# Bucketed attention and a rational feed-forward layer: partial sums merged by an adding transfer, four additions per pair moved to DVE

## The chip, the core and the metric

The kernel runs on one core of a Trainium2 chip. The time is that of the device, in microseconds, from the first to the last work of the core; the median of several runs is compared, and one execution is recorded by the hardware profiler. PE is the engine that multiplies matrices, DVE, ACT and POOL work on tiles of 128 partitions, and SP issues most of the transfers.

## The reference

```python
B, H, S, D = 4, 8, 768, 64
q_bucket = sum((q @ proj > 0) * 2 ** arange(6))        # k_bucket likewise
scores = where(q_bucket == k_bucket, q @ k.T / 8, -1e9)
attn = exp(scores - max(scores))
attn = attn / (sum(attn) + 1e-9)
x = (attn @ v) as (3072 tokens, 512)
h = x @ w_in                                            # 512 -> 2048
P = a0 + a1 h + a2 h^2 + a3 h^3
Q = 1 + |b0| |h| + |b1| h^2
out = (P / (Q + 1e-6)) @ w_out                          # 2048 -> 512
```

Queries see the keys of their own bucket alone. What the change touches is `sum(attn)`: for each query, the sum of the exponentials over all 768 keys, which later divides the values.

## The kernel before

The 32 heads are worked on as 16 pairs (`p`), two heads (`h`) side by side. For a pair the 768 keys are six tiles of 128 (`kt`) and the 768 queries two halves of 384 (`hf`); twelve steps `s` (`hf`, `kt`) make a pair. A step multiplies one tile of keys with one half of the queries, for both heads (`pss`, two products each), ACT takes the exponential into one of seven buffers `E`, and later PE multiplies it with the values (`psv`, twelve products in a row per half). In the same twelve steps PE also makes the twelve products for the maxima of the pair two ahead (`psm`, into two buffers), which DVE reduces one by one (`m`). In every second pair the bucket bits of two coming pairs are made (`psb`, eight products; DVE's comparison `mb`).

The sums over keys have two stages. The six exponentials of a half are added element by element in two parts of three tiles (`PARTS`): `acc = E + E`, then `acc = acc + E`, for each head, so four additions for one part of one half and sixteen for a pair. POOL makes them all, but for nine in the last pairs that DVE makes. A part is one tile `acc` of 128 partitions by two heads by 384, from a pool of five (`ACCS`). Then `sums` lets PE add over the 128 partitions: it multiplies `acc` with a matrix of ones into `psu`, eight products for a pair (two parts, two halves, two heads), the second part added to the first in PSUM. ACT copies the result (`sr`), SP stores it, and after four pairs `recips` reads it back and DVE takes the reciprocals.

Around this the weights of the feed-forward layer are split into two parts (`wr`, `ws`, `wi_hi`, `wi_lo`, on ACT and DVE), and the queries and keys of coming pairs too (`lo` on DVE). The feed-forward layer follows from about 400 us to the end.

Each engine works in the order in which its instructions are written. That order comes from a plan: `at(p, s, f, ...)` puts the call `f` at step 12 p + s, and the calls are made in the order of these numbers. The tables `MID` (pairs in the middle), `FIRST` and `LAST` hold the steps. In `MID`, `sums` stands at 14.65, that is 2.65 steps after the pair's last step, and `sums_store` at 17.37.

Of the kernel before, what the change touches and what calls it, by code (L numbers as in the profile page):

```python
# [7 lines left out]
F32 = mybir.dt.float32  # L8
# [5 lines left out]
ALU = mybir.AluOpType  # L14
# [4 lines left out]
P = 128  # L19
S = 768  # L20
HQ = 384
NT = S // P
# [3 lines left out]
NPAIR = B * NHP  # L26
# [11 lines left out]
PARTS = 2  # L38
ACCS = 5

MID = dict(
    group=6, values=[0.66, 0.05], values_out=3.5, maxima=7.17,
    maxima_steps=[0, 1.15, 1.73, 2.64, 3.32, 5.08, 5.86, 6.98, 8.0, 8.84, 10.26, 11.37], sums=14.65, sums_store=17.37,
    high=[-0.41, 1.19], low=[1.06, 3.35], bits=2.81, penalties=4.05, high_move=1.9, maskrows=5.61, second_low=-2.2,
    second_high=2.69, load_v=10.99, shift_turn=8.61, shift_rows=8.82, load=9.0, recips=[20.0, 22.0, 23.0],
    weights=[[1.44, 4.0, 4.1, 5.09, 5.49, 7.11, 9.5, 9.75, 17.5], [8.05, 10, 10.65, 11.5, 12.38, 14.29, 16.34, 19.32, 21.22]],
    weights_last=[0.5, 0.8, 1.0, 1.2],
)

FIRST = dict(  # L50
    maxima1=4.62, rate1=0.45, maxima2=9.5, rate2=0.82, high=[3.25, 3.53], low=[6.0, 7.3], bits=7.15, penalties=7.25,
    high_move=4.53, maskrows=8.2, second_low=4.25, second_high=4.35, load_v=4.78, group=2,
    values=[2.35, 2.65, 2.32, 2.35, 0.35, 0.61], values_out=3.02, high1=[-0.27, -5.58], low1=[11.24, 4.95],
    high_move1=20.05, load2=21.89, load3=-1.5, penalties1=-6.57, maskrows1=3.69,
    weights=[[-5.7, 6.64, 6.7, 11.42, 12.19, 18.75, 21.75, 38.77, 44.13], [8.03, 9.04, 9.24, 11.12, 14.81, 15.27, 15.99, 17.91, 46.81]],
    warm=6, warms=[3, 3, 3, 1, 1, 1], maxima00=[-4.26, -2.29, -4.17, 1.67, -1.15, 2.77], shift00=[2.15, 4.99],
    shift0=[3.67, 3.44], ahead=3, scores=[[3.68, 3.82, 7.26], [6.03, 8.25, 12.4]], pen01=[4.77, 14.55], comp01=3.35,
    second_high0=[-2.86, 2.12, -3.42, 3.45], load_v0=20.9, bits1=5.23, comp1=[15.82, 11.68],
    maxima0=[3.11, -1.97, -0.5, 2.14, 2.86, 3.25], turn1=[8.46, 13.26], rows1=[9.59, 14.35],
)  # L60

LAST = dict(
    group=6, values=[0.28, 0.44], values_out=1.39, vout14=3.03,
    tokens=[[-7.43, -5.11, -2.83, -1.09], [-0.04, 3.83, 9.38, 9.53]], terms=7.05, ffn=[13.61, 16.09, 16.14],
    sums=16.96, wide=8, share=11, third=0, sums14=14.69, sumst14=22.46,
)
# [99 lines left out]
def attention(ctx, tc, nc, raw, ps_b, tail, tokens, early, operands_to_terms, ffn, load, QF, KF, v, w_in, w_out, wo_d, ident, cst, ones, prj,  # L166
# [9 lines left out]
    sm = ctx.enter_context(tc.tile_pool(name="sm", bufs=1))  # L176
# [169 lines left out]
    def scores(p, s, heads=(0, 1)):  # L346
# [35 lines left out]
    def values_out(p, hf):  # L382
        ps = AV.pop((p, hf))
        col = sm.tile([P, 1], F32, tag="col", name=f"col{p}_{hf}")
        xo = AV[p, hf] = tail.tile([P, HQ], F32, tag="xo", name=f"xo{p}_{hf}", bufs=2)
        nc.scalar.copy(col, ps[:, HQ : HQ + 1])
        nc.scalar.activation(xo, ps[:, 0:HQ], AF.Identity, bias=col)

    def values_store(p, hf):
        nc.sync.dma_start(x_d[p][:, hf * HQ : hf * HQ + HQ], AV.pop((p, hf)))  # L390

    def sums(p):
        ps = ps_b.tile([P, 512], F32, tag="s", bufs=3, name=f"psu{p}")
        for k in range(PARTS):
            for hf in range(2):
                acc = ACC.pop((p, hf, k))
                for h in range(2):
                    o = 64 * h + 32 * hf
                    nc.tensor.matmul(ps[o : o + 32, 0:HQ], ones, acc[:, h, :], start=(k == 0), stop=(k == PARTS - 1))
        ACC[p] = tail.tile([P, HQ], F32, tag="sr", name=f"sr{p}")  # L400
        nc.scalar.copy(ACC[p], ps[:, 0:HQ])
# [69 lines left out]
    def at(p, s, f, *args):  # L471
        plan.setdefault(12 * p + s, []).append((f, args))

    def spread(p, steps, gen):
        for s in steps:
            at(p, s, lambda g: next(g, None), gen)

    for p in range(NPAIR):
        mid = 0 < p < NPAIR - 1
        n = MID["group"] if mid else (FIRST if p == 0 else LAST)["group"]  # L480
        for s in range(12):
            if p > 0 or s >= FIRST["ahead"]:
                at(p, s, scores, p, s)

            if p > 1:
# [8 lines left out]
        if p < NPAIR - 1:  # L494
            at(p, MID["sums"] if p < NPAIR - 2 else LAST["sums14"], sums, p)
            at(p, MID["sums_store"] if p < NPAIR - 2 else LAST["sumst14"], sums_store, p)
        if p > 1:
# [82 lines left out]
    at(0, FIRST["load3"], load, 3)  # L580
    spread(1, (0, 2), coefficients())
    for g in sorted(plan):
# [224 lines left out]
```

## Time and profile before

| | |
|---|---|
| Median of 3 runs | 946.7 us (946.19 to 948.16) |
| Profiled execution | 946.58 us, span 944.8 us |
| PE busy | 935.3 us, 99% |
| DVE busy | 868.6 us, 92% |
| ACT busy | 678.8 us, 72% |
| POOL busy | 442.7 us, 47% |
| Products of the sums (psu) | 256 records of PE, 24.0 us |
| POOL's additions into acc | 247 instructions, 291.1 us |
| DVE's additions into acc | 9 instructions, 10.0 us |
| PE's granted clock | 1.00 in the attention |

An engine's busy time is the time in which at least one of its instructions ran. PE's products overlap, and one product of 32-bit numbers that are not rounded beforehand is two records, so 256 records of psu are 128 products. In the lines of the profile a group reads: line, engine, operation, output and inputs, shape, count, then busy time and mean duration in ns, then the idle time of the engine before it and who ended it. Nearly all instructions carry the line of a helper, so groups are told apart by the names of their tiles. A timeline's row reads: start, duration, engine, instruction, count. A wait's row reads: who waited for whom, total, times, longest.

### The profile page before, as it was taken

The numbers are of one execution on the slowest core, as the hardware profiler recorded it, in microseconds if no ns is written. First come the engines' busy times: TensorE is split into PE (matmuls) and PEld (weight loads), VectorE is DVE, ScalarE is ACT, GpSimd is POOL, SyncE is SP. The second block draws the span as 40 slices with busy tenths as digits, with TensorE's granted clock in tenths as the row PEclk, the third lists the DMA queues.
The fourth block names the chain that finished last, engine by engine and source line by source line (L and its number), as shares of the span: only waits on it lengthen the run. The fifth ranks groups of instructions, "written<-read, shape, count | busy, mean of one in ns | idle before, by whom it ended". The sixth has DMA issues, their size and how long they took to land.

```text
span 944.8 us, 14848 instructions
## 1 busy us (share of the span) xinstructions
PE 935.3 (99%) x5062; PEld 752.0 (80%) x5062; DVE 868.6 (92%) x1217; ACT 678.8 (72%) x1419; POOL 442.7 (47%) x394
## 2 busy tenths in 40 slices
PE   8999999999999999999999999999999999999997
PEld 4666666666667676589989989989899899899996
DVE  6799889888988897899999999999999999999996
ACT  7577767667667676787777787777777777777765
POOL 5587878777778787512222222222222222222222
PEclk9999999999999999999999999999999999999999
DMA  7677878787777767456021021021110110210000
GB/s 212 193 199 207 235 216 239 208 221 221 227 220 225 226 192 215 130 205 252 1 68 34 1 68 34 1 67 34 39 47 17 66 36 1 67 34 1 34 1 34
DMA packets 50032, 111.65 MB, mean 118 GB/s; under 512 B 9154, under 2 KB 22070, under 8 KB 49956
## 3 DMA queue, kind: packets, MB, share of 16 engines
q1 hardware_dynamic: 49524, 110.47, 39.4%
q8 instruction: 40, 0.66, 0.3%
q14 instruction: 36, 0.29, 0.1%
q10 hardware_dynamic: 432, 0.23, 0.1%
HBM read 56.82 MB, written 21.17 MB: 83 GB/s over the span
## 4 chain that ended last, share of the span: by engine, by line
PE 91%; DVE 4%; DMA 2%; ACT 1%; SPq 1%; issue 1%; ACTq 0%; DVEq 0%
PE psh L89 28%; PE pso L89 28%; PE pss L89 12%; PE psv L89 11%; PE psm L89 7%; DVE m L89 2%; PE psu L89 2%; DMA wr<-w_in 2%; PE psb L89 1%; ACT E L89 1%; SPq L89 1%; DVE ws L89 1%; DVE wr L89 0%; DMA kf<-kT 0%; DVE lo L89 0%
## 5 line engine op out<-in xcount | busy, mean ns | idle before, releaser
L89 POOL TENSOR_TENSOR gl<-c,gh 128x384 fp32r<-128x384 f32 x128 | 141.3, 1104 | 395.9 <-ACT gh L89 375.7
L89 ACT ACTIVATE E<-pss 128x384 f32<-128x384 f32 x384 | 167.8, 493 | 108.7 <-PE pss L89 94.6
L89 PE MATMUL pso<-wo,gh 128*128 128x512 f32 x768 | 240.5, 395 | 0.0
L89 DVE TENSOR_REDUCE m<-psm 128x1 f32<-128x768 f32 x192 | 179.5, 948 | 34.3 <-PE psm L89 31.0
L89 POOL TENSOR_TENSOR acc<-E,E 128x384 f32<-128x384 f32 x124 | 154.6, 1267 | 88.6 <-ACT E L89 88.4
L89 PE MATMUL psh<-xl,wi_hi 128*128 128x384 f32 x512 | 172.1, 336 | 0.0
L89 PE MATMUL psh<-xh,wi_hi 128*128 128x384 f32 x512 | 171.7, 335 | 0.0
L89 PE MATMUL pss<-q,k 128*128 128x384 f32 (+2 forms) x768 | 170.9, 346 | 0.7 <-ACT col L89 0.4
L89 PE MATMUL psh<-xh,wi_lo 128*128 128x384 f32 x512 | 171.5, 335 | 0.0
L89 PEld LDWEIGHTS pso<-wo,gh 128*128 128x128 f32 x768 | 142.8, 188 | 23.9
L89 PEld LDWEIGHTS pss<-q,k 128*128 128x128 f32 (+2 forms) x768 | 134.6, 189 | 29.3 <-issue 17.0
L89 ACT ACTIVATE h<-psh 128x384 f32<-128x384 f32 x128 | 63.1, 493 | 126.0 <-PE psh L89 125.9
L89 PE MATMUL pso<-wo,gl 128*128 128x512 f32 x384 | 151.3, 396 | 0.0
L89 DVE SCALAR_TENSOR_TENSOR c<-c,ab,r 128x384 f32<-128x384 f32 x128 | 148.6, 1161 | 0.0
L89 POOL TENSOR_TENSOR acc<-acc,E 128x384 f32<-128x384 f32 x123 | 136.5, 1129 | 7.7 <-ACT E L89 7.5
L89 PE MATMUL psv<-E,v 128*64 128x385 f32 x768 | 133.1, 492 | 0.8 <-ACT E L89 0.7
L89 PEld LDWEIGHTS psv<-E,v 128*64 128x64 f32 x768 | 52.4, 136 | 67.1 <-issue 62.8
L89 PE MATMUL psm<-k,q 76*128 76x384 f32 (+1 forms) x384 | 102.4, 349 | 1.9 <-DVE m L89 1.0
L89 PEld LDWEIGHTS psh<-xh,wi_hi 128*128 128x128 f32 x512 | 96.1, 188 | 6.3 <-issue 1.2
L89 PEld LDWEIGHTS psh<-xl,wi_hi 128*128 128x128 f32 x512 | 96.0, 188 | 5.1
L89 PEld LDWEIGHTS psh<-xh,wi_lo 128*128 128x128 f32 x512 | 96.1, 188 | 0.0
L89 ACT ACTIVATE c<-psh,ab 128x384 f32<-128x384 f32 x128 | 86.5, 676 | 0.4 <-POOL gl L89 0.3
(81 smaller groups left out, 1288.5 us busy)
## 6 DMA issues: line engine op xcount, KB each, us to landing
q<-q SPq DMA_DIRECT2D x45, 192.0 KB
k<-k SPq DMA_DIRECT2D x45, 192.0 KB
wr<-w_in SPq DMA_DIRECT2D x16, 512.0 KB
wr<-w_out SPq DMA_DIRECT2D x16, 512.0 KB
wo_d<-wr SPq DMA_DIRECT2D x16, 512.0 KB
wo<-wo_d SPq DMA_DIRECT2D x16, 512.0 KB
qf<-qT SPq DMA_DIRECT2D x16, 384.0 KB
kf<-kT SPq DMA_DIRECT2D x16, 384.0 KB
```

The source lines that it names most:

```text
L89: return self.tc.keep_in_program_order(issue(*args, **kwargs))
```

## The change

In pairs 2 to 14 (`MERGED`) the two parts of a half are no longer both multiplied with ones. When both are complete, POOL issues a transfer from the second part's tile into the first part's tile that adds (`merge`), two per pair, 128 partitions by 768 numbers each. `sums` then makes four products instead of eight. In the same pairs the last addition of each part for the second head (`kt` 2 and 5, `h` 1) is taken from POOL and made by DVE 1.83 steps after the exponential's step (`add`), four per pair. The first parts have four buffers now and the second parts two, where all shared five; the output tile `xo` of the values has one buffer instead of two.

All tables of the order are rewritten. The sums of a pair stand at 19.5 instead of 14.65 and their store at 23.71 instead of 17.37; pairs 0 and 1 keep the old steps and the eight products, and pair 15 keeps eight products too.

```diff
-ACCS = 5
+ACCS = 4, 2
+MERGED = 2, NPAIR - 1
 MID = dict(
-    ... maxima_steps=[0, 1.15, 1.73, 2.64, 3.32, 5.08, ...], sums=14.65, sums_store=17.37, ... recips=[20.0, 22.0, 23.0],
+    ... maxima_steps=[0.79, 1.23, 1.75, 2.92, 3.18, 5.64, ...], sums=19.5, sums_store=23.71, ... recips=[31.16, 34.8, 44.46],
+    ... merge=[6.88, 7.36], dv=[2, 5], dvlag=1.83,
 ...
-            ACC[p, hf, kt // n] = sm.tile([P, 2, HQ], F32, tag="acc", name=f"acc{p}_{hf}_{kt // n}", bufs=ACCS)
+            ACC[p, hf, kt // n] = sm.tile([P, 2, HQ], F32, tag=f"acc{kt // n}", name=f"acc{p}_{hf}_{kt // n}", bufs=ACCS[kt // n])
 ...
             for h in heads:
-                engine = nc.vector if h and late >= LAST["share"] else nc.gpsimd
-                engine.tensor_tensor(out=acc[:, h, :], in0=x[:, h, 0:HQ], in1=e[:, h, 0:HQ], op=ALU.add)
+                if not (h == 1 and kt in MID["dv"] and MERGED[0] <= p < MERGED[1]):
+                    engine = nc.vector if h and late >= LAST["share"] else nc.gpsimd
+                    engine.tensor_tensor(out=acc[:, h, :], in0=x[:, h, 0:HQ], in1=e[:, h, 0:HQ], op=ALU.add)
+    def add(p, s):
+        hf, kt = divmod(s, NT)
+        acc = ACC[p, hf, kt // (NT // PARTS)]
+        nc.vector.tensor_tensor(out=acc[:, 1, :], in0=acc[:, 1, :], in1=EXP[p, s][:, 1, 0:HQ], op=ALU.add)
 ...
-        xo = AV[p, hf] = tail.tile([P, HQ], F32, tag="xo", name=f"xo{p}_{hf}", bufs=2)
+        xo = AV[p, hf] = tail.tile([P, HQ], F32, tag="xo", name=f"xo{p}_{hf}", bufs=1)
 ...
+    def merge(p, hf):
+        nc.gpsimd.dma_start(ACC[p, hf, 0], ACC.pop((p, hf, 1)), accum_op=ALU.add)
     def sums(p):
-        for k in range(PARTS):
+        n = 1 if MERGED[0] <= p < MERGED[1] else PARTS
+        for k in range(n):
 ...
+            if MERGED[0] <= p < MERGED[1] and s % NT in MID["dv"]:
+                at(p, s + MID["dvlag"], add, p, s)
 ...
+            for hf in range(2 if MERGED[0] <= p else 0):
+                at(p, 6 * hf + MID["merge"][hf], merge, p, hf)
```

On PE, before, in a pair that also makes bits, the four rows of psu (eight products) stand directly ahead of psb:

```order
L89 MATMUL psm_7_1512<-k_5_1225,q_5_1193 128x384 x2
L89 MATMUL psu_1521<-acc_0_0_1216,ones 32x384 x2
L89 MATMUL psu_1521<-acc_1_0_1355,ones 32x384 x2
L89 MATMUL psu_1521<-acc_0_1_1289,ones 32x384 x2
L89 MATMUL psu_1521<-acc_1_1_1427,ones 32x384 x2
L89 MATMUL psb_0_1537<-qf_1134,prj 32x384
```

On PE, now, the sums of a pair:

```order
L92 MATMUL pss_7_1_1340<-q_3_593,k_3_616 128x384
L92 MATMUL pss_7_1_1340<-q_3_891,k_3_892 128x384
L92 MATMUL psm_11_1347<-k_4_897,q_4_875 128x384 x2
L92 MATMUL psu_1355<-acc_0_0_937,ones 32x384 x2
L92 MATMUL psu_1355<-acc_1_0_1084,ones 32x384 x2
L92 MATMUL psm_0_1366<-k_5_1180,q_5_1159 128x384 x2
```

And, further on, the first bits:

```order
L92 MATMUL pss_3_0_1522<-q_4_875,k_4_897 128x384
L92 MATMUL pss_3_0_1522<-q_4_1174,k_4_1175 128x384
L92 MATMUL pss_3_1_1526<-q_4_875,k_4_897 128x384
L92 MATMUL pss_3_1_1526<-q_4_1174,k_4_1175 128x384
L92 MATMUL psb_0_1531<-qf_1091,prj 32x384
```

Four products are left, between two products of maxima, and sums and bits each stand alone.

On POOL, before, one pair's additions (the names are acc with half and part, `x2` is both heads):

```order
L89 TENSOR_TENSOR acc_0_0_934<-E_151,E_152 128x384 x2
L89 TENSOR_TENSOR acc_0_0_934<-acc_0_0_934,E_153 128x384 x2
L89 TENSOR_TENSOR acc_0_1_1018<-E_154,E_148 128x384 x2
L89 TENSOR_TENSOR acc_0_1_1018<-acc_0_1_1018,E_149 128x384 x2
L89 TENSOR_TENSOR acc_1_0_1085<-E_150,E_151 128x384 x2
```

On POOL, now, from the end of one pair into the next:

```order
L92 TENSOR_TENSOR acc_1_1_1148<-E_153,E_154 128x384 x2
L92 TENSOR_TENSOR acc_1_1_1148<-acc_1_1_1148,E_148 128x384
L92 TENSOR_TENSOR acc_0_0_1221<-E_149,E_150 128x384 x2
L92 DMA acc_1_0_1084<-acc_1_1_1148 128x768
L92 TENSOR_TENSOR acc_0_0_1221<-acc_0_0_1221,E_151 128x384
L92 TENSOR_TENSOR acc_0_1_1271<-E_152,E_153 128x384 x2
L92 TENSOR_TENSOR acc_0_1_1271<-acc_0_1_1271,E_154 128x384
L92 DMA acc_0_0_1221<-acc_0_1_1271 128x768
```

Every second row has one addition instead of two, and a transfer stands in POOL's order twice per pair, with the next part's additions behind it.

On DVE, now, from the last maxima of one pair to the first of the next:

```order
L92 TENSOR_REDUCE m_1915<-psm_10_2167 128x1
L92 TENSOR_TENSOR acc_0_1_2108<-acc_0_1_2108,E_148 128x384
L92 TENSOR_REDUCE m_1915<-psm_11_2185 128x1
L92 TENSOR_REDUCE m_2203<-psm_0_2204 128x1
L92 TENSOR_SCALAR mt_None<-pst_None 12x128
L92 TENSOR_REDUCE m_2203<-psm_1_2226 128x1
L92 TENSOR_REDUCE m_2203<-psm_2_2231 128x1
L92 TENSOR_TENSOR acc_1_0_2182<-acc_1_0_2182,E_151 128x384
L92 TENSOR_REDUCE m_2203<-psm_3_2256 128x1
```

Before, no addition stood among these rows; now one stands before the last maximum and one behind the third of the next pair.

More of the change, by code (lines that the diff above doesn't have):

```diff
@@ L38 @@
 PARTS = 2
-ACCS = 5
+ACCS = 4, 2
+MERGED = 2, NPAIR - 1
 MID = dict(
[L42 to L47, printed above, removed]
+    group=6, values=[0.88, 0.46], values_out=3.05, maxima=7.2,
+    maxima_steps=[0.79, 1.23, 1.75, 2.92, 3.18, 5.64, 6.46, 7.46, 9.63, 10.01, 11.6, 12.15], sums=19.5,
+    sums_store=23.71, high=[-1.36, -0.64], low=[2.93, 4.66], bits=3.12, penalties=4.08, high_move=2.8, maskrows=6.75,
+    second_low=-0.71, second_high=6.38, load_v=0.59, shift_turn=8.23, shift_rows=8.41, load=7.35,
+    recips=[31.16, 34.8, 44.46],
+    weights=[[2.04, 4.32, 5.15, 5.84, 6.36, 10.64, 12.29, 15.57, 21.18], [7.54, 10.93, 11.1, 11.86, 12.09, 16.33, 17.02, 18.99, 29.59]],
+    weights_last=[0.5, 0.8, 1.0, 1.2], merge=[6.88, 7.36], dv=[2, 5], dvlag=1.83,
@@ L48 @@
 )
 FIRST = dict(
[L51 to L59, printed above, removed]
+    maxima1=4.33, rate1=0.49, maxima2=9.99, rate2=0.85, high=[2.05, 3.05], low=[4.04, 4.31], bits=5.25, penalties=6.9,
@@ L60 @@
+    shift0=[3.61, 3.85], ahead=3, scores=[[1.64, 4.9, 6.35], [9.05, 9.85, 12.0]], pen01=[6.11, 12.34], comp01=3.58,
+    second_high0=[-0.26, -1.65, -0.72, 7.24], load_v0=21.14, bits1=6.71, comp1=[10.88, 16.35],
+    maxima0=[0.97, -4.4, -0.96, 2.75, 3.35, 3.25], turn1=[7.62, 12.38], rows1=[10.53, 15.94], coef=[-0.5, 20.9],
+    sums=14.65, sums_store=17.37,
 )
@@ L64 @@
     tokens=[[-7.43, -5.11, -2.83, -1.09], [-0.04, 3.83, 9.38, 9.53]], terms=7.05, ffn=[13.61, 16.09, 16.14],
-    sums=16.96, wide=8, share=11, third=0, sums14=14.69, sumst14=22.46,
+    sums=16.96, wide=8, share=11, third=0, sums14=18.5, sumst14=22.46,
 )
@@ L398, in sums @@
                     o = 64 * h + 32 * hf
-                    nc.tensor.matmul(ps[o : o + 32, 0:HQ], ones, acc[:, h, :], start=(k == 0), stop=(k == PARTS - 1))
+                    nc.tensor.matmul(ps[o : o + 32, 0:HQ], ones, acc[:, h, :], start=(k == 0), stop=(k == n - 1))
         ACC[p] = tail.tile([P, HQ], F32, tag="sr", name=f"sr{p}")
```

12 lines of the change are left out of this document (9 added, 3 removed).

## The prediction

> **What bounds the kernel now.** I read the page first (busy shares, slices, chain of waits), then the busy time by stage, then the groups and waits of the stage that the change touches, and last the timeline at the places where the four products of the sums stand.
>
> ```profile
> PE 935.3 (99%) x5062; PEld 752.0 (80%) x5062; DVE 868.6 (92%) x1217; ACT 678.8 (72%) x1419; POOL 442.7 (47%) x394
> DVE  6799889888988897899999999999999999999996
> POOL 5587878777778787512222222222222222222222
> PE 91%; DVE 4%; DMA 2%; ACT 1%; SPq 1%; issue 1%; ACTq 0%; DVEq 0%
> ```
>
> PE is the chain: 91% of it, busy 99% of the span. But DVE stands at eight to nine tenths through the attention (slices 1 to 16) and POOL at seven to eight tenths, so a microsecond taken off PE is worth something only as long as DVE keeps up. The stage with thirteen like pairs shows it. The sums of pair 1 begin at 76.3 us and those of pair 13 at 362.3 us, so this window is twelve pairs (columns: PE, PE's weight loads, DVE, ACT and POOL busy, clock, DMA share, GB/s):
>
> ```profile
> 0.00:52.18 52.18, 49.26 (x258) 29.44 (x259) 37.33 (x54) 32.25 (x57) 30.47 (x37) 1.00 0.70 200
> 76.30:362.30 286.00, 285.70 (x1744) 197.47 (x1743) 254.57 (x298) 199.96 (x450) 226.85 (x193) 1.00 0.76 218
> 362.30:407.90 45.60, 44.18 (x262) 29.67 (x262) 35.20 (x42) 33.41 (x77) 25.99 (x23) 1.00 0.52 160
> ```
>
> 286.00 / 12 = 23.83 us per pair. PE is busy 285.70 of 286.00: it hardly waits. DVE is busy 21.21 us per pair and idle 2.62; POOL is busy 18.90; the DMA engines 0.76 of the time at 218 GB/s. Who waits for whom in that window:
>
> ```profile
> DVE m L89 <- PE psm L89: 22.0, 19, 2.4
> ACT E L89 <- POOL acc L89: 10.7, 4, 3.6
> PEld psm L89 <- DVE m L89: 3.5, 13, 0.5
> ```
>
> DVE waits for PE (22.0 us), and PE's weight loads for DVE only 3.5 us. So PE sets the pace, and DVE follows with little to spare.
>
> **The change, part by part.** *Taken from PE.* A sum of a pair is eight products now (two parts, two halves, two heads), four in the thirteen merged pairs. The timeline of PE shows one beside the bits of a coming pair and one without:
>
> ```profile
> 267.40 1.50 PE L89 MATMUL psu<-acc,ones 128*32 128x384 f32 x16
> 268.72 0.49 PE L89 MATMUL psb<-qf,prj 128*32 128x384 f32 x2
> 291.26 0.51 PE L89 MATMUL psm<-k,q 76*128 76x384 f32 x2
> 291.71 1.50 PE L89 MATMUL psu<-acc,ones 128*32 128x384 f32 x16
> 293.14 0.98 PE L89 MATMUL pss<-q,k 77*128 77x384 f32 x4
> ```
>
> Eight products hold PE for 268.72 - 267.40 = 1.32 us. Half of them go: 0.66 us per pair, 13 x 0.66 = 8.6 us. (Half of the group's busy time would be 0.75; its ends run under the next products, so I take the distance of the starts.) Something comes back: in six places the sums and the bits no longer stand side by side on PE, and each such group alone costs an entry and an exit. Exit: 293.14 - 291.71 = 1.43 instead of 1.32, 0.11 us. Entry: two products of psm take 0.51 us, so the second starts 0.17 after the first, at 291.43, and psu 0.28 later instead of 0.17: 0.11 us. 6 x 0.22 = 1.3 us. PE's own work falls by 7.3 us, 0.56 per pair: PE could run a pair in 23.27 us.
>
> *Added to DVE.* Four additions per pair, 52 in all. DVE makes nine such additions now, in the last pairs, and their groups and three single ones, with the POOL instruction beside the first, read:
>
> ```profile
> L89 DVE TENSOR_TENSOR acc<-acc,E 128x384 f32<-128x384 f32 x5 | 5.6, 1115 | 0.6 <-ACT E L89 0.5
> L89 DVE TENSOR_TENSOR acc<-E,E 128x384 f32<-128x384 f32 x4 | 4.4, 1093 | 1.4 <-ACT E L89 1.4
> 384.58 1.38 DVE L89 TENSOR_TENSOR acc<-E,E 128x384 f32<-128x384 f32 x1
> 384.19 1.35 POOL L89 TENSOR_TENSOR acc<-acc,E 128x384 f32<-128x384 f32 x1
> 386.06 0.56 DVE L89 TENSOR_TENSOR acc<-acc,E 128x384 f32<-128x384 f32 x1
> 388.83 0.55 DVE L89 TENSOR_TENSOR acc<-E,E 128x384 f32<-128x384 f32 x1
> ```
>
> Alone an addition takes 0.55 us (386.06 and 388.83, while POOL stands still); while POOL adds, it waits for POOL to finish and then makes its own (384.58 + 1.38 = 385.96, POOL's ends at 385.54). DVE's instructions overlap by about 0.09 us (176.03 to 176.89 below is 0.86 for 0.95), so the price is 0.46 at least and 1.02 at the mean of the nine. Which, depends on how often POOL is at work. DVE's other work shows what that costs today, in the same window:
>
> ```profile
> L89 DVE SCALAR_TENSOR_TENSOR ws<-ws,wr 128x512 int32<-128x512 int32 x24 | 31.3, 1306 | 0.4
> L89 DVE TENSOR_TENSOR wr<-ws,wr 128x512 fp32r<-128x512 f32 x12 | 17.1, 1425 | 0.0
> L89 DVE TENSOR_TENSOR wi_lo<-ws,wi_hi 128x512 fp32r<-128x512 f32 x12 | 14.0, 1163 | 0.0
> L89 DVE TENSOR_TENSOR lo<-kf,k 128x768 fp32r<-128x768 f32 x12 | 13.6, 1130 | 0.0
> 390.34 0.68 DVE L89 TENSOR_TENSOR wr<-ws,wr 128x512 fp32r<-128x512 f32 x1
> 176.03 0.95 DVE L89 TENSOR_TENSOR lo<-kf,k 128x768 fp32r<-128x768 f32 x1
> 176.89 0.95 DVE L89 TENSOR_REDUCE m<-psm 128x1 f32<-128x768 f32 x1
> ```
>
> With 0.68 as the time alone of the first three and 0.95 of the fourth, DVE stands blocked 24 x 0.63 + 12 x 0.75 + 12 x 0.48 + 12 x 0.18 = 32 us, 2.7 us per pair. POOL's additions read so:
>
> ```profile
> L89 POOL TENSOR_TENSOR acc<-E,E 128x384 f32<-128x384 f32 x97 | 123.4, 1293 | 59.7 <-ACT E L89 59.4
> L89 POOL TENSOR_TENSOR acc<-acc,E 128x384 f32<-128x384 f32 x96 | 107.0, 1135 | 2.0 <-ACT E L89 1.9
> 386.94 1.00 POOL L89 TENSOR_TENSOR acc<-E,E 128x384 f32<-128x384 f32 x1 [1.40 <-ACT E L89]
> ```
>
> Sixteen per pair at 1.00 us alone are 16.0 of 23.8 us, 67%; the change leaves twelve, 12.0 of 23.3, 52%. So a new addition on DVE meets POOL about half the time and then waits half an instruction: 0.46 + 0.52 x 0.5 = 0.72 us, 2.9 per pair; and the old blocked time shrinks with POOL's share, 2.7 x (1 - 52/67) = 0.6. DVE: 21.2 + 2.9 - 0.6 = 23.5 us per pair. The bounds: 21.2 + 4 x 0.46 - 0.6 = 22.4 (every addition alone) and 21.2 + 4 x 1.02 = 25.3 (the mean of the nine, no relief). The middle is already above the 23.27 of PE. The order puts the additions between maxima (behind psm_2, and between psm_10 and psm_11): there PE's next psm needs the maximum behind the addition, two buffers on, so a late DVE is at once a late PE. I take 23.55 us per pair: 0.28 above what PE could do, 13 x 0.28 = 3.6 us given back.
>
> *Taken from POOL, added to it.* Four additions at 1.14 us go, 4.5 us per pair; two issues of a transfer come. No row shows what POOL pays for one. Below, an issue could cost nothing; above, POOL has 23.3 - (18.9 - 4.5) = 8.9 us per pair to give, 4.4 per issue, before it binds. I take it as covered by POOL's idle time. Behind the first transfer of a pair stand the additions of the next half, and the transfer itself waits for DVE's addition; if they are late, the buffers of E are late for ACT. The 10.7 us in four waits of ACT for POOL above cost PE nothing visible (0.30 us idle in the window), so there is cover of that size.
>
> [...]
>
> The slack: the second half's transfer is placed at step 13.36 and the sums at 19.5, a step being 23.8 / 12 = 2.0 us: 12 us. I cost its landing at nothing.
>
> *The transfers' load.* Each carries 128 x 768 x 4 bytes = 393 KB. The engines move 218 / 0.76 = 287 GB/s at full share, so 1.4 us each, 2.7 us per pair; the share rises from 0.76 to (18.1 + 2.7) / 23.3 = 0.89. If an adding transfer moves its bytes twice, 5.5 us: 1.01, no room. No row shows an adding transfer; I take once, and keep twice and more for a rival.
>
> *The rest.* All tables of the order are new, also for pairs 0, 1 and 15, one xo buffer goes, the sums' results come five steps later. PE idles 2.9 us up to 52.18 and 1.4 us from 362.3 to 407.9, so no more than 4.3 us can be won there; as much could be lost. I take nothing. Behind 407.9 the work is untouched.
>
> Sum: -8.6 + 1.3 (entries) + 3.6 (given back by DVE, 13 x (23.55 - 23.27)) = -3.7. The profiled execution took 946.58 us (span 944.8, the rest lies around it), so 942.9; it stands 0.1 under the median of 946.7, so for a median **943.0 us**.
>
> **The rivals.**
>
> 1. *PE keeps all of it* (chance 0.20): DVE's additions fall into its 2.62 us of idle time and POOL's relief pays for their waits (22.4 per pair, under 23.27). For it: DVE waits 22.0 us for PE. Against: those waits stand where the maxima arrive, not where the additions do. 946.6 - 7.3 = 939.3 us.
>
> 2. *No change* (0.18): DVE takes 23.7 to 23.95 per pair, and the gain is eaten. 946 us.
>
> 3. *DVE becomes the bound* (0.25). Place: the maxima that follow an addition. Price: at 1.02 us each, less the 0.6, DVE is 21.2 + 4.1 - 0.6 = 24.7; between that and the 23.83 of today lies 24.3: 13 x 0.5 = +6, 952.6 us (at 24.7: 958). It decides from an addition of 0.8 us on. For it: the mean of all nine rows is 1.1. Against: eight of these stand where POOL adds the other head at the same moment, released by the same ACT.
>
> 4. *The transfers fill the DMA engines* (0.07): at three times their bytes 8.2 us per pair, 26.3 in all, 13 x 2.5 = +32, 979 us at worst; at twice, loads come late by little and the pair stays near 24, 949 us. Against: 0.24 of the time is free today.
>
> **How the numbers follow.** The forecast has 0.30, the largest. About 0.2% (1.9 us) is what can be told from no change. Faster: 0.30 + 0.20 = 0.50; same 0.18; slower 0.25 + 0.07 = 0.32. The likeliest case's own range is 941 to 944.7 (pairs of 23.4 to 23.68 us). For 8 in 10 the range reaches from below rival 1 (938.5) to rival 3 at its middle (952.5), which leaves out half of rival 3 and most of rival 4.
>
> **What would show it.** PE's psu group should fall from 256 to 152 records and by 8 to 10 us busy. DVE's acc group should show 52 more, at 0.55 to 1.4 us, mean near 0.8, and DVE should be busy over 23 us of a pair. The ws and wr groups should come down from 1306 and 1425 ns. POOL's additions should number 16 per pair less four, and ACT's waits for POOL not grow. The DMA share should rise to about 0.89; a rise past 0.95 with waits of ACT or PE for transfers speaks for rival 4. If PE's waits for DVE's maxima stay near 3.5 us, rival 1 is right; if PE's idle or stretched time between psm products passes 0.56 us per pair, rival 3. A POOL row of an issue longer than 4 us, or psu waiting for a transfer, would make the covers wrong that I counted on.

## The result: 36 us slower

The changed kernel takes 983.4 us (median of 4 runs, 981.2 to 990.7) against 947.1 us for the kernel before (946.2 to 948.2). The ratio is 1.040, 95% interval 1.037 to 1.043: slower by 36 us, far outside the range I gave. The profiled execution is one of 981.19 us, with a span of 979.4.

From the page of the changed kernel (engines; slices of DVE, POOL and the granted clock; the chain):

```profile
PE 952.1 (97%) x4958; PEld 755.7 (77%) x4958; DVE 919.4 (94%) x1268; ACT 687.3 (70%) x1419; POOL 386.1 (39%) x369
...
DVE  6889999999999799889999999999999999999997
...
POOL 5676554455565364542222222222222222222222
PEclk9999999999999797999999999999999999999999
...
PE 76%; DVE 12%; issue 5%; DMA 3%; ACT 2%; SPq 1%; POOL 0%; DVEq 0%; ACTq 0%; POOLq 0%
```

PE has 104 records fewer, which are 52 products, as announced, and yet it is busy 17 us longer. The chain of waits shows why to look elsewhere: PE's share fell from 91% to 76%, and DVE's rose from 4% to 12%. In two slices the granted clock stands at 7 tenths, where the windows of before all had 1.00.

Busy time of the eleven pairs from the sums of pair 2 (113.66) to those of pair 13 (406.35), PE, weight loads, DVE, ACT, POOL, clock, DMA share, GB/s:

```profile
113.66:406.35 292.69, 277.68 (x1500) 184.59 (x1500) 275.59 (x316) 189.00 (x410) 157.29 (x154) 0.95 0.83 224
```

Nearly the same stretch of the kernel before, the columns alike:

```profile
100.10:362.30 262.20, 261.90 (x1594) 181.06 (x1592) 234.01 (x275) 183.36 (x413) 208.25 (x177) 1.00 0.77 219
```

292.69 / 11 = 26.6 us per pair, where the eleven pairs took 23.8 each before. DVE is busy 25.05 us of a pair, and PE is idle for 15.0 us of the window, 0.3 before. For whom they wait, in the window of the changed kernel:

```profile
POOL acc L92 <- DVE acc L92: 65.4, 11, 8.1
...
PEld psm L92 <- DVE m L92: 28.3, 37, 2.3
...
PE psm L92 <- DVE m L92: 11.1, 18, 2.0
```

PE's products waited 11.1 us for DVE's maxima, 1.0 us per pair. PE's weight loads waited 28.3 us for them, against 3.5 us in twelve pairs before. The two can't be added: PE as a whole was idle for 15.0. And POOL waits for DVE's addition up to 8.1 us at a time. The groups of DVE's instructions with two inputs in SBUF, POOL's issue of the transfer, and the sums:

```profile
L92 DVE TENSOR_TENSOR acc<-acc,E 128x384 f32<-128x384 f32 x56 | 65.1, 1162 | 1.7 <-POOL acc L92 1.0 <-ACT E L92 0.4
L92 DVE TENSOR_TENSOR lo<-qf,q 128x768 fp32r<-128x768 f32 x13 | 37.1, 2857 | 0.0
...
L92 DVE SCALAR_TENSOR_TENSOR ws<-ws,wr 128x512 int32<-128x512 int32 x32 | 22.7, 708 | 0.5
...
L92 DVE TENSOR_TENSOR wr<-ws,wr 128x512 fp32r<-128x512 f32 x16 | 12.3, 772 | 0.1
...
L92 POOL DMA_DIRECT2D acc<-acc x26 | 22.8, 875 | 76.3 <-DVE acc L92 76.3
...
L92 PE MATMUL psu<-acc,ones 128*32 128x384 f32 x152 | 15.6, 496 | 0.0
```

The row of before that my prediction did not look at, since the change does not touch that instruction:

```profile
L89 DVE TENSOR_TENSOR lo<-qf,q 128x768 fp32r<-128x768 f32 x13 | 12.6, 968 | 0.6 <-DMA q<-lo 0.6
```

lo from qf is the same subtraction in both kernels, and it went from 0.97 to 2.86 us. The work with wr and ws became shorter, by more than predicted (tables_only below bears on why); something new holds up lo. The timeline of DVE and POOL at one of the thirteen places:

```profile
365.64 2.68 DVE L92 TENSOR_REDUCE m<-psm 128x1 f32<-128x768 f32 x3
368.24 5.10 DVE L92 TENSOR_TENSOR lo<-qf,q 128x768 fp32r<-128x768 f32 x1
373.27 0.55 DVE L92 TENSOR_TENSOR acc<-acc,E 128x384 f32<-128x384 f32 x1
...
367.73 0.85 POOL L92 DMA_DIRECT2D acc<-acc  x1
368.34 1.29 POOL L92 TENSOR_TENSOR acc<-acc,E 128x384 f32<-128x384 f32 x1
369.32 2.25 POOL L92 TENSOR_TENSOR acc<-E,E 128x384 f32<-128x384 f32 x2
371.27 1.25 POOL L92 TENSOR_TENSOR acc<-acc,E 128x384 f32<-128x384 f32 x1
```

lo starts at 368.24, while POOL issues the transfer, and ends at 373.34: 0.8 us behind the fourth addition that POOL runs back to back behind the issue. Its own work is 0.95. Until then DVE made no maxima, and POOL's next transfer then waited for DVE's addition. My theory from this trace, **S**: behind a transfer's issue POOL runs its queued additions with no two-input instruction of DVE in between, so that such an instruction waits for POOL's next pause (here 5.10 us for 0.95) and not, as before, for one POOL instruction (1.38 us for an addition of 0.55 at 384.58 in the kernel before).

### The profile page after: what moved, and what is told of

It reads as the page before. It is cut to its first block, busy times and chain, and to the rows that moved or that the text cites. A ratio compares the mean times of both kernels' runs of the same rounds, so it can differ in the third digit from the quotient of the medians.

```text
span 979.4 us, 14789 instructions
## 1 busy us (share of the span) xinstructions
PE 952.1 (97%) x4958; PEld 755.7 (77%) x4958; DVE 919.4 (94%) x1268; ACT 687.3 (70%) x1419; POOL 386.1 (39%) x369
## 3 DMA queue, kind: packets, MB, share of 16 engines
q0 software_dynamic: 3744, 10.23, 5.7%
## 4 chain that ended last, share of the span: by engine, by line
PE 76%; DVE 12%; issue 5%; DMA 3%; ACT 2%; SPq 1%; POOL 0%; DVEq 0%; ACTq 0%; POOLq 0%
PE pso L92 27%; PE psh L92 27%; PE psv L92 9%; PE pss L92 8%; DVE m L92 6%; PE psm L92 4%; DVE lo L92 2%; DVE acc L92 2%; ACT E L92 1%; DVE wr L92 1%; DMA wr<-w_out 1%; DMA qf<-qT 1%; DVE ws L92 1%; SPq L92 1%; DMA x<-x_d 1%
## 5 line engine op out<-in xcount | busy, mean ns | idle before, releaser
L92 DVE TENSOR_REDUCE m<-psm 128x1 f32<-128x768 f32 x192 | 176.0, 947 | 16.4 <-PE psm L92 15.5
L92 PE MATMUL pss<-q,k 128*128 128x384 f32 (+2 forms) x768 | 178.0, 359 | 1.5 <-ACT E L92 0.7
L92 POOL TENSOR_TENSOR acc<-E,E 128x384 f32<-128x384 f32 x124 | 137.6, 1187 | 80.3 <-ACT E L92 80.2
L92 PEld LDWEIGHTS pss<-q,k 128*128 128x128 f32 (+2 forms) x768 | 140.6, 198 | 30.9 <-issue 20.4
L92 PE MATMUL psm<-k,q 76*128 76x384 f32 (+1 forms) x384 | 106.5, 368 | 16.4 <-DVE m L92 13.7
L92 POOL TENSOR_TENSOR acc<-acc,E 128x384 f32<-128x384 f32 x72 | 89.2, 1242 | 30.4 <-ACT E L92 30.2
L92 PEld LDWEIGHTS psm<-k,q 76*128 76x128 f32 (+1 forms) x384 | 67.7, 196 | 41.1 <-DVE m L92 35.7
```

Of the source, the lines that this page charges most:

```text
L92: return self.tc.keep_in_program_order(issue(*args, **kwargs))
```

## The experiments

The expectations of the first four runs call S T1, with the further condition that POOL first stood waiting behind DVE's addition. Rivals to S: the additions on DVE are dear by themselves (T2 below), the transfers as such, by issue or traffic (T3), their traffic (D, later C), the bunching of POOL behind DVE's addition, without any transfer (B), and the order of the new tables (T4, T; later O, the order that is left). Times are medians, ratios to the kernel before with 95% intervals; "per pair" is the time from the sums of pair 2 to those of pair 13, divided by eleven.

### Parts of the change apart

tables_only:

```diff
-ACCS = 4, 2
+ACCS = 6
...
-    sums=19.5, sums_store=23.71, recips=[31.16, 34.8, 44.46], sums14=18.5, dv=[2, 5],
+    sums=14.65, sums_store=17.37, recips=[20.0, 22.0, 23.0], sums14=14.69, dv=[],
...
-        n = 1 if MERGED[0] <= p < MERGED[1] else PARTS
+        n = PARTS
...
-            for hf in range(2 if MERGED[0] <= p else 0):
+            for hf in range(0):
```

> The new tables of the order alone: no transfer, no addition moved to DVE; all sums have eight products again, at step 14.65, and the accumulators share one tag of six buffers. Theory T1 (a POOL queue that stood behind DVE's addition runs its additions without a pause, DVE's two-input instructions starve behind them, PE stalls and its clock halves): needs both parts of the change, so 945 to 953 us, clock 1.0, no addition or lo of DVE over 2.5 us. Theory T2 (the four additions per pair are simply dear on DVE): 945 to 953. Theory T3 (the transfers themselves, their issue on POOL or their traffic): 945 to 953. Theory T4 (the new tables are a bad order on the chip, whatever the change): 965 to 985.

Measured: 959.0 us, 1.013 (1.011 to 1.014). The new tables alone cost 12 us, more than any theory but T4 had, and less than the 18 to 38 that T4 needs. One more thing is to be seen here: POOL makes all its additions as before, and yet ws takes 725 ns and wr 860, against 1233 and 1342 in the whole run before.

tables_dve is the same with `dv=[2, 5]`:

> The new tables with DVE's four additions per pair, without the transfers: eight products per sum, as in tables_only. T1: POOL never waits for DVE here, so no train of POOL instructions follows such a wait: additions of 0.6 to 1.1 us, 948 to 960 us, lo from qf under 2 us in the mean. T2: as slow as the change or slower (PE has 8.6 us more to do): 980 to 992 us. T3: equal to tables_only within 5 us. T4: 975 to 990.

Measured: 988.6 us, 1.045 (1.040 to 1.049). No instruction of DVE is held up by more than 0.9 us, and an addition takes 0.70 us in the mean. That is the price that I had predicted, and yet the time is 29 us above tables_only, in the ranges of T2 and T4; S expected 948 to 960 and missed. Its trace has stretches such as this one:

```profile
302.60:306.00 3.40, 2.34 (x13) 1.58 (x11) 3.40 (x5) 2.13 (x6) 2.88 (x3) 1.00 0.99 302
306.00:316.20 10.20, 10.09 (x31) 7.10 (x32) 6.45 (x10) 6.13 (x12) 3.85 (x4) 0.50 0.37 112
```

PE stands 1.06 us in 3.4, and then its clock is granted at 0.50 for 10.2 us. I come back to this.

tables_merge is the change with `dv=[]`, old_tables_merge the same with the tables of before (the sums stay at 19.5):

```diff
-    weights_last=[0.5, 0.8, 1.0, 1.2], merge=[6.88, 7.36], dv=[2, 5], dvlag=1.83,
+    weights_last=[0.5, 0.8, 1.0, 1.2], merge=[6.88, 7.36], dv=[], dvlag=1.83,
```

> The change with all additions left on POOL (the transfers stay, four products per merged sum, DVE makes no addition in the thirteen pairs). T1: the transfer waits for POOL's own additions alone, so POOL never stands behind DVE: 938 to 952 us, POOL's waits for DVE gone (76 us now), clock at least 0.995. T2: 937 to 943 us, PE keeps its 7.3 us. T3: nearly as slow as the change, 970 to 985 us, lo from qf again near 2.9 us in the mean. T4: 960 to 980 us.

> The tables of before with the transfers alone (sums at step 19.5, the transfer at 6.88 and 13.36; all additions on POOL). T1: 938 to 950 us, below tables_merge or equal to it within 5. T2: 938 to 943. T3: 970 to 985, as tables_merge. T4: 938 to 945, and far below tables_merge.

Measured: 1011.6 us, 1.066 (1.061 to 1.071), and 993.6 us, 1.047 (1.042 to 1.053). Both are slower than any theory had them, and T3 came nearest. So the transfer does the damage without any addition on DVE, and more of it; T2 falls as the main cause. S missed too, in what it took for needed: POOL need not wait for DVE. The hold is there with the longer train. DVE and POOL in tables_merge:

```profile
224.10 7.12 DVE L92 TENSOR_TENSOR lo<-qf,q 128x768 fp32r<-128x768 f32 x1
...
224.00 0.87 POOL L92 DMA_DIRECT2D acc<-acc  x1
224.61 2.11 POOL L92 TENSOR_TENSOR acc<-acc,E 128x384 f32<-128x384 f32 x2
226.41 2.23 POOL L92 TENSOR_TENSOR acc<-E,E 128x384 f32<-128x384 f32 x2
228.33 2.07 POOL L92 TENSOR_TENSOR acc<-acc,E 128x384 f32<-128x384 f32 x2
230.70 0.87 POOL L92 DMA_DIRECT2D acc<-acc  x1 [0.30 <-POOL acc L92]
```

Six additions without a pause, and lo takes 7.12 us; it ends at 231.22, 0.82 us after POOL's last addition (230.40). In old_tables_merge it is lo from kf that stands there, up to 6.39 us.

### What of the transfer it is

marker, tiny_transfer and sync_copy replace the transfer of the change by something else at the same place (the new lines slightly shortened; the name behind each is that of its kernel):

```diff
-        nc.gpsimd.dma_start(ACC[p, hf, 0], ACC.pop((p, hf, 1)), accum_op=ALU.add)
+        nc.gpsimd.tensor_copy(ACC[p, hf, 0][:, :, 0:1], ACC.pop((p, hf, 1))[:, :, 0:1])      # marker
+        nc.gpsimd.dma_start(ACC[p, hf, 0][:, :, 0:1], ACC.pop((p, hf, 1))[:, :, 0:1])        # tiny_transfer
+        nc.sync.dma_start(ACC[p, hf, 0], ACC.pop((p, hf, 1)))                                # sync_copy
```

> The change with each transfer replaced by a copy of 128 x 2 elements on POOL, at the same place, from and to the same tiles, so that POOL waits for DVE exactly as before; the sums keep four products. It leaves out the second part of every merged sum (and adds 1 instead of a tiny constant before the reciprocal). [...] Theory B (it is POOL's bunching behind DVE's addition alone): excesses of 2 to 5 us remain on lo and on the additions, 970 to 985 us. Theory T (the order of the new tables): 970 to 985 without such excesses.

> The change with a plain transfer of 128 x 2 elements issued on POOL in place of the adding one of 128 x 768 (the second part of every merged sum is left out, as in marker). Theory S, by the issue: excesses of 2 to 5 us as in the change, 970 to 985 us. [...] Theory B: as the change, 970 to 985.

> The change with a plain transfer of the whole 128 x 768 issued on SyncE's queue (it writes over the first part, so the first part of every merged sum is left out): POOL neither issues nor waits for DVE. Theory S: no excess over 0.95 us on DVE, 945 to 965 us. Theory D: excesses remain, 965 to 985. Theory B: no excess, 945 to 965. If SyncE's waiting for DVE's addition holds up the loads behind it, waits for q, k or wr grow and it takes 965 or more without excesses.

By S, marker was to take 950 to 965 us, with no instruction of DVE held by over 0.95 us, since it issues nothing; by D, tiny_transfer the same, since it moves next to nothing.

Measured: marker 951.4 us, 1.005 (1.004 to 1.006); tiny_transfer 974.0, 1.027 (1.020 to 1.033), its four runs from 965.6 to 978.8; sync_copy 999.1, 1.056 (1.050 to 1.061). The first two are the pair that decides. marker has the same order on every engine, the same waits of POOL for DVE and the same train of additions:

```profile
346.34 0.95 DVE L92 TENSOR_TENSOR lo<-qf,q 128x768 fp32r<-128x768 f32 x1
347.20 1.36 DVE L92 TENSOR_TENSOR acc<-acc,E 128x384 f32<-128x384 f32 x1
...
346.25 0.18 POOL L92 COPY acc<-acc 128x2 f32<-128x2 f32 x1
346.39 1.76 POOL L92 TENSOR_TENSOR acc<-acc,E 128x384 f32<-128x384 f32 x1
348.12 3.00 POOL L92 TENSOR_TENSOR acc<-E,E 128x384 f32<-128x384 f32 x2
```

Here the two take turns: lo has its 0.95 us, POOL's addition waits (1.76 instead of 1.0), then DVE's. tiny_transfer moves 1 KB in place of 384 KB:

```profile
357.89 5.39 DVE L92 TENSOR_TENSOR lo<-qf,q 128x768 fp32r<-128x768 f32 x1
...
357.80 0.72 POOL L92 DMA_DIRECT2D acc<-acc  x1
358.55 1.02 POOL L92 TENSOR_TENSOR acc<-acc,E 128x384 f32<-128x384 f32 x1
359.52 1.98 POOL L92 TENSOR_TENSOR acc<-E,E 128x384 f32<-128x384 f32 x2
361.45 1.00 POOL L92 TENSOR_TENSOR acc<-acc,E 128x384 f32<-128x384 f32 x1
```

lo is held for the whole train, with next to no bytes moved. So it is the issue on POOL: S stands, B and (for this part) D fall. The ten kernels that issue transfers on POOL have 439 instructions of DVE for lo or acc<-acc,E between 60 and 450 us. 104 of them began during an issue or in the additions that followed one without a pause of 0.15 us: 55 of these were held by more than 1 us, by up to 6.2, and 49 were not (held means longer than the shortest of the kind in the same run). The other 335 were held by 0.90 us at most.

S speaks of two-input instructions, and that is too narrow: of 20 instructions that change wr in place (one input) and began there, four were held by more than 1 us, one by 4.4 (in old_later at 383.97 us). DVE's maxima, which read PSUM, were not held: 264 began there, and none took over 0.03 us more than the shortest.

sync_copy has no hold (0.87 at most) and is the slowest of the three: SyncE's queue then waits for DVE's addition (57.9 us in the pairs), and what stands behind it comes late. ACT waited 19.0 and 12.2 us for wr from w_out and from w_in. That was the side condition in its expectation.

### The place of the issue

merge_in_pause is old_tables_merge with one number changed; change_later is the change, old_later is merge_in_pause, each with the transfers two steps on:

```diff
-  merge=[6.88, 7.36]
+  merge=[6.88, 6.88]      # merge_in_pause, on old_tables_merge
+  merge=[8.88, 8.88]      # change_later on the change; old_later on merge_in_pause
```

> old_tables_merge with one number changed: the second half's transfer at step 12.88 instead of 13.36, so that on POOL it stands ahead of the next half's first two additions, in the pause in which POOL waits for ACT, and no longer between them and the next four. Theory S: the train behind it is broken by the wait, the 5.4 us excesses of lo from kf go, 940 to 960 us, clock at least 0.99. Theory D and theory B: no difference from old_tables_merge within 8 us of 993.6.

> The change with both transfers two steps later (8.88 and 14.88 instead of 6.88 and 13.36): on POOL each stands between the additions of steps 2 and 4 of the next half, where POOL waits for ACT, and DVE's addition that it needs is two steps older. Theory S: POOL's waits for DVE's addition fall from 76 us to under 20, no DVE instruction is held up by more than 1 us in most pairs, clock at least 0.995, 952 to 965 us (marker took 951.4, and some of the 9 us between tiny_transfer and the change comes back as traffic). If the loss of the change has another cause than the place of the issue: 975 to 990.

> merge_in_pause with both transfers two steps later (8.88 and 14.88): the second half's then stands behind the load of the weights of w_in (1.44 of the next pair) and ahead of lo from kf (3.35). Theory C: ACT's waits for wr from w_in fall under 15 us; theory S: DVE is held up by over 1.5 us only where POOL's additions follow without a pause, in fewer than half of the pairs. Together 948 to 965 us. Theory O: 968 to 980.

Measured: merge_in_pause 973.5 us, 1.027 (1.024 to 1.030); change_later 981.4, 1.033 (1.027 to 1.039), one of its four runs at 970.0; old_later 993.9, 1.047 (1.041 to 1.053). The first confirms S: no instruction is held by more than 0.9 us, and 20 us of 47 are gone by moving one of a pair's two issues from behind two additions to ahead of them. It does not confirm my number (940 to 960): 26 us are left. change_later took as long as the expectation gave for another cause than the place of the issue (975 to 990). POOL's waits for DVE are gone there, but DVE's own addition now stands beside the issue and is held by 1.9 to 2.9 us in six of the pairs. The hold moved and did not go; my expectation had reckoned with POOL's waits only. In old_later, slower than either theory had it, few instructions are held (four by over 1.5 us, three of them those on wr), other things come late, and I did not settle which of them weighs.

### The traffic

```diff
-        nc.gpsimd.dma_start(ACC[p, hf, 0], ACC.pop((p, hf, 1)), accum_op=ALU.add)
+        nc.gpsimd.dma_start(ACC[p, hf, 0][:, :, 0:1], ACC.pop((p, hf, 1))[:, :, 0:1])        # tiny_in_pause
+        nc.gpsimd.dma_start(ACC[p, hf, 0], ACC.pop((p, hf, 1)))                              # plain_in_pause
-    weights=[[1.44, 4.0, 4.1, ...
+    weights=[[-0.6, 4.0, 4.1, ...                                                            # loads_earlier
```

> merge_in_pause with each adding transfer replaced by a plain one of 128 x 2 elements issued on POOL at the same place (the second part of the merged sums is left out). The issue stays, the traffic goes. Theory C: ACT's waits for wr from w_in fall under 10 us, 938 to 950 us. Theory O: 965 to 978 us. If the issue on POOL alone costs time even in a pause, without starving DVE: 955 to 965.

> merge_in_pause with a plain transfer of the same 128 x 768 issued on POOL in place of the adding one (it writes over the first part, so that is left out of the merged sums). If the traffic costs because it adds: packets of 3072 bytes at half of 252 ns, the DMA share in the pairs down from 0.91 to 0.84, 955 to 963 us. If the bytes do it: packets as long as the adding ones, 968 to 976 us.

> merge_in_pause with one number changed: the load of the weights of w_in at step -0.6 instead of 1.44, ahead of the second half's transfer instead of behind it. Theory C (what is left of the loss in merge_in_pause, 26 us, is the transfer's traffic in front of the weights' load: ACT waited 36.7 us for wr from w_in): that wait falls under 10 us and the time to 945 to 960 us. Theory O (what is left is the order alone: sums later, the rest of the tables untouched): 968 to 978 us.

Measured, all on merge_in_pause (973.5): tiny_in_pause 953.8 us, 1.007 (1.005 to 1.008); plain_in_pause 959.0, 1.013 (1.010 to 1.016); loads_earlier 970.3, 1.025 (1.023 to 1.027). So 19.7 us go with the traffic, and 14.5 of them with the adding (the plain transfer's issue is shorter too, 0.56 us against 0.88). The adding had its range right (955 to 963); tiny_in_pause lies between the ranges of C and of the issue alone. The queue of these transfers in the adding and in the plain kernel (packets, MB, share of 16 engines):

```profile
q0 software_dynamic: 3744, 10.23, 5.7%
```

```profile
q0 software_dynamic: 2080, 10.23, 3.1%
```

The same bytes take 5.7% of 972.8 us, or 55 us, of the sixteen engines when added, and 30 when copied. The eleven pairs of merge_in_pause and ACT's waits for the weights in them (total, times, longest), and then the same two rows of tiny_in_pause:

```profile
113.52:398.68 285.16, 272.16 (x1498) 181.86 (x1498) 213.94 (x271) 185.95 (x409) 216.35 (x199) 0.96 0.91 232
```

```profile
ACT ws L91 <- DMA wr<-w_in: 31.5, 11, 6.0
```

```profile
110.97:379.27 268.30, 260.86 (x1499) 176.44 (x1498) 226.95 (x272) 184.33 (x410) 215.85 (x198) 0.99 0.76 213
```

```profile
ACT ws L91 <- DMA wr<-w_in: 4.9, 4, 2.5
```

With the traffic the DMA share is 0.91 instead of 0.76, and the weights come late to ACT, which works in the order written: the exponentials behind them are late, and PE waits (idle 13.0 us of these pairs, 7.4 in tiny_in_pause). loads_earlier shows that this is part of it: ACT's wait falls from 31.5 to 13.2 us, and its pairs take 24.99 us instead of 25.92, ten us in eleven pairs. The kernel gains 3 only: pair 2's sums come 6.6 us later (120.07 instead of 113.52). I put that down to its first load, which now stands in the way at the start; a mended start was not tried, so this is not shown. My expectation of 945 to 960 was wrong, and the time lies in the range of O (968 to 978).

### What PE's four products are worth

half_sums is the kernel before without the products of the second parts:

```diff
         for k in range(PARTS):
             for hf in range(2):
                 acc = ACC.pop((p, hf, k))
+                if merged and k > 0:
+                    continue
...
```

The one_part kernels have one chain of five additions per half and head in the thirteen pairs, so four products and no transfer. They differ in what DVE makes of the second head's additions: in dve4 those of kt 4 and 5, in dve2 that of kt 5, each 1.83 steps on; in pool none; in gap those of steps 10 and 11, at step 12.2. Of the edit against the kernel before:

```diff
-        n = NT // PARTS
+        merged = MERGED[0] <= p < MERGED[1]
+        n = NT if merged else NT // PARTS
...
```

> The kernel before with the four products of the second parts left out of the sums of the thirteen pairs, nothing moved (it leaves out half of every merged sum, and adds 1 instead of a tiny constant before the reciprocal). If PE sets the pace, as the prediction's first term has it: 947 - 8.6 = 938.5 us, 937.5 to 940.5. If another loop of engines (DVE, ACT, POOL) holds a pair at 23.8 us whatever PE saves, as the runs with four products suggest (24.1 to 24.4 us per pair without transfers): 944 to 947.5.

> As one_part_dve4 with all twenty additions on POOL, none moved to DVE. By the terms: POOL 18.9 + 4 x 1.1 = 23.3 per pair against 23.2 on PE, so POOL is full and E comes free late: ACT waits for POOL over 30 us, 950 to 965 us. If PE's relief shows all the same: 938 to 946.

> one_part_pool with two additions per pair on DVE, the last two of the second head in the second half, placed at step 12.2, where DVE waited about 2 us for PE in seven of ten pairs of before. If these two fit into the gap and POOL with eighteen additions is no longer full: 939 to 945 us. If DVE's additions hold up PE's next maxima even there: 950 to 965 us, with psm or psu waiting for DVE by over 0.5 us per pair.

> Tables of before, no transfer: in the thirteen pairs each half and head has one chain of five additions, so a sum has four products at its old step 14.65; DVE makes the last two additions of the second head, POOL sixteen per pair as before. If a microsecond off PE is worth a microsecond while DVE's additions cost 0.7 to 0.8 us (my prediction's terms): PE 8.6 us less, DVE 21.2 + 4 x 0.75 = 24.2 per pair, so 946 to 953 us. If DVE's additions stall PE's maxima wherever they stand: 960 to 975 us with windows at half clock.

> As one_part_dve4 with the last addition of the second head alone on DVE (two per pair); POOL makes eighteen. By the terms of the prediction: DVE 21.2 + 1.6 + 0.3 (POOL busier) = 23.1 and POOL 18.9 + 2.3 = 21.2 of PE's 23.2 per pair: 938 to 946 us. If POOL's lateness holds up the buffers of E: ACT's waits for POOL over 15 us and 950 to 965 us.

Measured: half_sums 943.1 us, 0.996 (0.994 to 0.998); one_part_pool 948.7, 1.002 (1.001 to 1.003); one_part_gap 948.9, 1.003 (1.001 to 1.004); one_part_dve4 970.6, 1.025 (1.021 to 1.029); one_part_dve2 968.9, 1.023 (1.020 to 1.027). Of the five only one_part_dve4 lies in a range of its expectation (960 to 975). The saving alone brings 3.9 us, between 2.2 and 5.5, not the 8.6 of the distances of the starts. The pairs of half_sums (its profiled execution, 940.5 us, is the fastest of twelve), and of one_part_pool:

```profile
100.07:356.77 256.70, 255.18 (x1500) 177.42 (x1499) 233.26 (x274) 182.83 (x412) 208.25 (x177) 1.00 0.78 223
```

```profile
100.65:364.82 264.17, 260.30 (x1500) 177.16 (x1499) 235.44 (x274) 183.14 (x412) 247.17 (x221) 1.00 0.76 216
```

In the first, a pair takes 23.3 us, with PE busy all but 0.14 of each. In the second POOL is busy 22.5 of 24.0: full, as expected. one_part_gap and the two others show how little room DVE has: two additions in its idle stretch cost nothing against one_part_pool but gain nothing, and the same two in other places cost 20 us. In one_part_dve4 PE waits for the maxima (eleven pairs):

```profile
PEld psm L90 <- DVE m L90: 16.4, 14, 1.5
...
PE psm L90 <- DVE m L90: 11.7, 13, 1.2
```

PE is idle 12.3 us in these pairs, and 11.7 of it are these waits of its products. No version that computes the whole result beat the kernel before.

## Why the prediction was wrong, step by step

The runs make a ladder from 947.1 to the change:

| from, to | us | what is added |
|---|---|---|
| before, half_sums | -3.9 | four products fewer |
| half_sums, marker | +8.3 | new tables, sums five steps later, DVE's additions |
| marker, tiny_transfer | +22.6 (single runs 14 to 27) | the issue of a transfer on POOL |
| tiny_transfer, the change | +9.4 | its bytes, and that it adds |

**Taken from PE: mis-sized.** I took 8.6 us; alone it is worth 3.9. The products went as forecast, from 256 records to 152. Where the other half goes I can't show; PE's rows merely fill the time.

**Added to DVE: right alone, wrong in company.** I took 0.72 us per addition; without transfers it is 0.69 (marker) and 0.70 (tables_dve). In the change it is 1.16, over the point (0.8) from which my third rival was to decide. The relief came, and larger than my 0.6 us per pair, but not for my reason: over the whole run ws fell from 1233 to 708 ns and wr from 1342 to 772, yet tables_only has 725 and 860 with every addition left on POOL. So most of it goes with the new tables and not with POOL's smaller share. The loss came from holds: 13 x (2.86 - 0.97) = 24.5 us of DVE's time on lo, which my sum left out, and 65.1 - 38.9 = 26.2 us on the additions, against those of marker.

**Taken from POOL, added to it: the step that failed.** I wrote "I take it as covered by POOL's idle time". POOL's time was indeed covered: an issue took 0.88 us, POOL was busy 39%, and ACT's waits for POOL did not grow. But the price of an issue is paid by DVE: marker has none and takes 951.4 us, tiny_transfer has 26 and takes 974.0. I bounded it by POOL's own idle time from both sides, though no row showed an issue. The bound from above that the runs show is what stands on POOL behind the issue, one to five additions in the change, for an instruction of DVE on SBUF that begins beside them: up to 4.6 us a time.

In the change no issue took over 1.01 us, and it was DVE that waited. In the ten kernels without an issue on POOL, lo and the additions were held by 0.91 us at most; behind an issue by up to 4.2 us over four POOL instructions, and 6.2 over six.

**The landing: mis-sized.** "I cost its landing at nothing" looked at the sums, and they indeed never waited for the transfer. The others on the DMA engines did: 9.4 us in the change, 19.7 in the kernel with the transfer in the pause. Of my two estimates for its time, 2.7 us per pair if the bytes go once and 5.5 if twice, the trace has 5.7% x 979.4 / 13 = 4.3.

**The clock: not in the sum at all.** I priced a stall at its own length. In the change at 373 to 381 us, PE's rows, and the windows before and behind:

```profile
375.61 0.61 PE L92 MATMUL psm<-k,q 76*128 76x384 f32 x2 [0.37 <-DVE m L92]
...
377.41 0.62 PE L92 MATMUL psm<-k,q 76*128 76x384 f32 x2 [0.48 <-DVE m L92]
...
379.70 0.62 PE L92 MATMUL psm<-k,q 76*128 76x384 f32 x2 [0.89 <-DVE m L92]
```

```profile
376.85:380.26 3.41, 2.04 (x14) 1.01 (x14) 3.27 (x6) 1.17 (x3) 0.00 (x0) 1.00 0.63 199
380.27:390.50 10.23, 10.23 (x34) 8.13 (x34) 8.37 (x15) 6.20 (x13) 6.80 (x7) 0.50 0.48 129
```

1.37 us of idle time in 3.41, and the clock is granted at 0.50 for 10.2 us: up to 5 us more for 1.4 of stall. The change has five such drops, 30.7 us at half clock, or 15 us of PE's time. Four of them, 27.3 us, lie in the eleven pairs. These became 30 us longer: PE was idle for 15 of it, and busy 16 longer with 44 products fewer; half of the 27.3, 13.7 us, is the clock. How much of that reaches the end can be estimated from two executions of one kernel: tiny_transfer took 965.6 us at a mean clock of 0.997 and 978.8 at 0.980, 13.2 us for 0.017 x 975 = 16.6 us of lost clock. By that 0.8, up to 12 of the 36 us are the clock: up to, since an execution with more drops also has more of the stalls that go before them. They are part of the ladder's steps and not beside them.

**The order.** "I take nothing" for the new tables: tables_only took 12 us more, with eight products and without the rest. How the 8.3 us from half_sums to marker divide between tables, sums and additions is open (in marker DVE is busy 22.3 us of a pair, less than my 23.5, and a pair still takes 24.2), and so is why tables_dve (988.6) is so far above marker (951.4) with the same additions: it has five drops of the clock, marker has none, but what first makes PE late there I did not separate.

**The signs and the range.** Of the signs I named, PE's waits for maxima decided rightly: 1.0 us per pair before its products against the bound of 0.56 for the third rival, DVE as the bound. That rival had the place right, but 952.6 to 958 for its price: without lo, the traffic and the clock. A POOL issue longer than 4 us, the sign I gave for a failing cover, did not come although the cover failed. The DMA share in the pairs rose to 0.83, less than 0.89, because the pairs became longer (0.83 x 26.6 = 22.1 us per pair, against my 20.8). My chance of 0.32 for slower was too small for an operation, the issue, that no row of the trace showed.

## What to carry to other kernels

Before a transfer is issued on POOL, look at what POOL has queued behind it and which instructions of DVE work on SBUF beside it: put the issue where POOL pauses next (no hold over 0.9 us in merge_in_pause), or the price can be the whole train (6.2 us over six additions in tables_merge). An operation that no row shows is not bounded by the idle time of the engine that issues it; ask which other engine's instructions grow longer beside it. And where PE is busy 99%, price a cluster of stalls also by what the clock does next (here 0.50 for 10.2 us after 1.37 us of idle time), not by its length alone.

## What the runs showed of the hardware that I had not expected

- **A hold over several instructions.** Behind a transfer issued on POOL, even of 1 KB, an instruction of DVE on SBUF that began during the issue or in the additions behind it could wait until POOL paused, up to 6.2 us over six additions: 55 of 104 for lo and the additions. DVE's maxima, read from PSUM, did not wait (0.03 us at most). A 128 x 2 copy on POOL at the same place did not hold DVE (lo from qf 0.95 us in the mean of marker, 2.86 in tiny_transfer). Why the issue has this effect, and why 49 were spared, no run shows.
- **The clock halved after windows in which PE was idle for only a part.** Every one of the drops to 0.50 during the attention, in all profiled runs, followed a stretch of 3.41 us, as long as the shortest drop, in which PE stood idle for 0.7 to 3.4 us in sum, mostly 1 to 2 (0.9 to 2.0 before the five of the change); in the kernel before no stretch behind its first 52 us had more than 0.71. They lasted 3.4, 6.8, 10.2 us or more (three of 3.41 and two of 10.24 in the change). Idle time alone does not decide: stretches with up to 2.0 us (sync_copy) were followed by none, and one_part_dve4 has several with 1.1 and no drop. PE need not stand still all through: in the rows above it worked for 2.04 us of the 3.41, and no single wait was over 0.89.
- **The adding transfers took 1.9 times the engines' time of the plain ones** of the same bytes, 10.23 MB (5.7% against 3.1% of spans of 972.8 and 956.5 us, 55 and 30 us).
